# Favor attention and a mixture layer on one core: the sign step keyed to the exp table, two more quarters of GEMM 2 in seven products, another written-out order

## The chip, the core and the metric

The kernel runs on 1 core of a Trainium2 chip. The metric is the device time of one execution in microseconds (us), lower is better. Before the change, three runs gave 1028.66, 1029.24 and 1030.05 us, median 1029.24.

## The reference

Two stages follow each other. Attention with random features: for 8 batches of 8 heads, 576 tokens and 64 channels,

```python
def phi(x):
    proj = np.einsum('bhsd,md->bhsm', x, omega)
    sq = np.sum(x * x, axis=-1, keepdims=True) / 2.0
    h = proj - sq
    h = h - np.max(h, axis=-1, keepdims=True)
    return np.exp(h) / np.sqrt(m)
num = np.einsum('bhsm,bhmd->bhsd', q_p, kv)      # kv = k_p' v, z = sum of k_p
den = np.einsum('bhsm,bhm->bhs', q_p, z)[..., None] + 1e-06
x = num / den
```

and then a two-layer part on the 4608 tokens with 512 channels and 2048 hidden units:

```python
h = x @ w_in
sp = np.maximum(h, 0.0) + np.log1p(np.exp(-np.abs(h)))
g = h * erf(sp)
return g @ w_out
```

Everything is float32; the weights arrive as 64-bit floats.

## The kernel before, in words

**Tiling.** Two heads form a pair; 32 pairs go through attention one after the other (`attention`: projection `ppq`/`ppk`, exponentials `fq`/`fk`, key-value sums `kvp`, transposes `pt` into `qh`, products `nd`, and a division into `xs`). The tokens are cut into six supers (`SUPERS`), 0 and 1 of 2 x 288 columns, 2 to 5 of 2 x 432. A super needs the batches that its tokens lie in, so pairs of later batches run between the matrix products of earlier supers.

**GEMM 1 and GEMM 2.** Each super passes four quarters (`q`) of the hidden units. A quarter is two granules: GEMM 1 fills `hs`, `chain` takes softplus, erf and the product with `hs` (the gate), and GEMM 2 of that quarter follows one quarter later on TensorE, so that GEMM 1 of the next quarter covers the elementwise work. Every float32 product is three matmuls, high x high, high x rest and rest x high. Tiles with h (`xh`, `gh`, `th`, `bh`) hold the high part, those with l the rest. GEMM 1 of supers 0 and 1 is eight plain products (`plain1`), in supers 2 to 5 it is a Strassen-Winograd scheme of seven (`gemm1`, banks `hX`, `hY`, `hZ`). GEMM 2 is plain (`gemm2`, banks `o`) where `blocked(b, q)` is false, and else seven products (`gemm2_blocks`, banks `oX`, `oY`, `oZ`), for which `pieces2` forms differences of the halves of the gated tile (`gs`) and splits seven halves instead of four into high and rest, and `make_sums` forms sums of the weight blocks (`R`, `S`, `c`), once, in the super before the first that needs them.

**Weights.** `make` turns each 64-bit unit (`st`) into high and rest: a sign and exponent step on ScalarE (`w_bias`, a Prelu into `wt`), two integer steps on VectorE, then the high part and the rest into `w`. It stores the result, and later uses fetch it.

**The order.** `build` lists operations with reads, writes, engine choices and due times (`plan`); `Plan.order` is a planner that walks a model clock and gives each engine its next ready operation by due time. What it writes out is each engine's program, and the engines then run in that order with semaphores between them. `JITTER` moves due times within given intervals by a hash; `LAG`, `DRAIN`, `GATES` and others are the planner's lags and dates. On ScalarE a chain takes a lock from its first softplus to its last erf: an operation that names an activation set other than the chain's is held back; one that names none may run in between.

Sections that the change and the prediction touch, by the line numbers of the profile: `FIRST2` and `blocked` (66 to 71), `order` (150), `JITTER` (323), `make` and its `pbias` operation (431, 438), `make_sums` (472), `chain` (790), `pieces2` (828), `gemm2_blocks` (874), `gemm2` (905), `w_bias` (1076). The engines' instructions all carry the line of one helper, L1015, so groups are told apart by tile names.

Of the kernel before, what the change touches and what calls it, by code (L numbers as in the profile page):

```python
# [20 lines left out]
B, H, S, D = 8, 8, 576, 64  # L21
# [41 lines left out]
            ("Y", "S4", "B22", (0, 1), 1),  # L63
            ("X", "A22", "T4", (1, 0), 0))

FIRST2 = (3, 3, 3, 3)


def blocked(b, q):

    return FIRST2[q] <= b < len(SUPERS) - (q == NQ - 1)


COST = dict(mm=0.132, proj=0.222, half=0.156, tr=0.109, kv=1.35, table=1.3)
BANDWIDTH = 270e3
LAG = {"T": 0.32725, "A": 0.2525, "V": 0.2605, "G": 0.3105, "S": 0.2904}
SLOTS = dict(w=8, g=11, u=2, f=2, mx=3, sq=3, v=1, qh=1, ql=1, kh=1, kl=1, xs=12, xh=2, xl=2,
             os=4, ps=8)
CAPS = dict(st=3, wt=1, ws=1, wp=2, cv=2, att=4, moe1=5, moe2=3, hs=4, gs=2, w=6, wsums=7)
# [26 lines left out]
class Plan:  # L106
# [43 lines left out]
    def order(self, slots, caps):  # L150
# [6 lines left out]
        for o in reversed(ops):  # L157
# [2 lines left out]
            for s in o.succ:  # L160
                due = min(due, s.due - dur - 0.4)
            o.due = due
        for k, (lo, hi, amp) in enumerate(JITTER):
            for o in ops:
                if lo <= o.due < hi:
                    o.due += amp * ((o.id * 7919 + k * 104729 + 17) % 1009 / 504.0 - 1.0)
# [45 lines left out]
        while True:  # L212
# [74 lines left out]
            while True:  # L287
                if kind == "idle":
                    idle[x] = True
                elif kind == "done":  # L290
                    for s in x.succ:
                        s.left -= 1
                        lag = 0.0 if x.eng != "S" and len(s.opts) == 1 and s.opts[0][0] == x.eng \
                            else LAG[x.eng]
                        s.ready = max(getattr(s, "ready", 0.0) if s.left >= 0 else 0.0, now + lag) \
                            if hasattr(s, "ready") else now + lag
                        if not s.left:
                            event(max(now, s.ready), "push", s)
                    event(now + LAG[x.eng], "free", x)
                elif kind == "free":  # L300
# [17 lines left out]
def whole_(n):  # L318
# [1 line left out]
    return n < WHOLE or WHOLE2[0] <= n < WHOLE2[1]  # L320


JITTER = ((0, 0, 0), (186.1, 206.1, 4), (0, 0, 0), (0, 0, 0), (0, 0, 0), (227.5, 727.5, 4),
          (648.5, 748.5, 1), (712.0, 762.0, 2), (574.9, 594.9, 8), (27.8, 47.8, 0.5), (390.5, 440.5, 8),
          (458.1, 558.1, 8), (876.3, 896.3, 2), (0, 0, 0), (616.6, 816.6, 1))
AHEAD = 40.56

SPANS = ((0, 288), (288, 288))

DRAIN = 2.0  # L330
DIVIDE = 4.0
WHOLE = 32
WHOLE2 = (0, 0)
LESS = []
ROWS = 8
PAIR = 8.0
FIRST = 11.5
LEAD = 30.0
START0 = 4 * FIRST + 5

GATES = 10.0
RESTS = 6.0
EARLY = (0, 0)
STARTS = ()
BY = 30.0
RPOOL = SPOOL = "g"
VOS = 5
TAIL = [("V", 0.69, -1e9)]
LATE = 40.0
LOADS = 1e9  # L350
GATES0 = 1e9
RESTS0 = 1e9
SQN = 4
SQG = -1e9
SQA = 4.0
WHG = 5.0
WBG = -1e9


def build(emit):  # L360
# [49 lines left out]
    def fetch(u, t, src, ks, n):  # L410
        pl.op("wfetch", [("S", 0.1, AHEAD)], lambda e: E.fetch(t.ap[:, ks[0]:ks[-1] + 1].bitcast(F32), src()),
              reads=[(stored[u], 0)], writes=[(t, (x, k)) for x in "hl" for k in ks],
# [18 lines left out]
    def make(u, t):  # L431

        nm = "_".join(str(c) for c in u)
        st = pl.tile("w", f"st{nm}", [P, HW, 2], I32, "st")
        pl.op("wload", [("S", 0.1, AHEAD)], lambda e: E.w_load(st, u),
              writes=[(st, "h"), (st, "l"), (t, "room")], size=P * HW * 8)
        w = pl.tile("ps", f"wt{nm}", [P, HW], I32, "wp")
        pl.op("pbias", [("A", 0.67, -1e9)], lambda e: E.w_bias(e, st, w),
              reads=[(st, "h")], writes=[(w, 0)])
        pl.op("ptail", TAIL, lambda e: E.w_tail(e, st), reads=[(st, "l")], writes=[(st, "l")])  # L440
        pl.op("pjoin", [("V", 0.68, -1e9)], lambda e: E.w_join(st, w), reads=[(st, "l"), (w, 0)],
              writes=[(w, 0)])
        parts(t, lambda: w.ap.bitcast(F32).rearrange("p (k c) -> p k c", k=2), [(w, 0)], True)
        store(u, t)

    def room():
        count[0] += 1
        if clock[0] < starts[SUMS]:
            return CAPS["w"]
        return CAPS["wsums"] if clock[0] < starts[max(SUMS + 1, *FIRST2)] else SLOTS["w"]  # L450

# [291 lines left out]
    def plain1(b, ph, fp):  # L743
# [5 lines left out]
        def one(i, t):  # L749
# [3 lines left out]
            for k in range(2):  # L753
                product(hp, where[f"A{i + 1}{k + 1}"], b, XPLAIN, f"B{k + 1}{t + 1}", k, k)
            pl.op("hout", [("A", d["A"], -1e9), ("V", d["V"], 0.0)],
                  lambda e: E.h_out(e, hs.ap[:, i, t, :], hp, T), reads=[(hp, 0)], writes=[(hs, (i, t))],
                  plan=clock[0] + DRAIN)
        return [lambda i=i, t=t: one(i, t) for i in range(2) for t in range(2)]
# [7 lines left out]
    def gemm1(b, ph, fp, where, srcs, which):  # L766
# [5 lines left out]
        def one(bank, wn, xn, to, plus):  # L772
# [6 lines left out]
            if plus:  # L779
                pl.op("hadd", [("V", d["V"], -1e9)], lambda e: E.h_add(hs.ap[:, to[0], to[1], :], hp, T),  # L780
                      reads=[(hp, 0), (hs, to)], writes=[(hs, to)], plan=clock[0] + DRAIN)
            else:
                pl.op("hout", [("A", d["A"], -1e9), ("V", d["V"], 0.0)],
                      lambda e: E.h_out(e, hs.ap[:, to[0], to[1], :], hp, T), reads=[(hp, 0)],
                      writes=[(hs, to)], plan=clock[0] + DRAIN)
        return [lambda x=x: one(*x) for x in PRODUCTS]
# [87 lines left out]
    def gemm2_blocks(b, q, j, where, srcs):  # L874
# [6 lines left out]
        def one(bank, wn, xn, to, plus):  # L881
# [10 lines left out]
            if plus or q:  # L892
                pl.op("oadd", [("V", d["V"], -1e9)], lambda e: E.o_add(o, op, t, T),
                      reads=[(op, 0), (o, t)], writes=[(o, t)], plan=clock[0] + DRAIN)
            else:
                pl.op("oout", [("V", d["V"], -1e9), ("A", d["A"], -1e9)],
                      lambda e: E.o_out(e, o, op, t, T), reads=[(op, 0)], writes=[(o, t)],
                      plan=clock[0] + DRAIN)
            if q == NQ - 1 and (to[0] == 0 and wn == "S4" or wn == "A22"):
# [5 lines left out]
    def gemm2(b, q, et):  # L905
# [7 lines left out]
        def out(t):  # L913
            if q == 0:
                pl.op("oout", [("V", d["V"], -1e9), ("A", d["A"], -1e9)],
                      lambda e: E.o_out(e, o, ops[t], t, T), reads=[(ops[t], 0)], writes=[(o, t)],
                      plan=clock[0] + DRAIN)
            else:
# [3 lines left out]
        def one(t, f):  # L922
            if not ops:
                ops.extend(pl.tile("ps", f"o{b}_{q}_{et}_{i}", [P, 512], F32, "moe2",
                                   6 if b == len(SUPERS) - 1 else None) for i in range(2))
                w.append(weights2(q // 2, et, q % 2))
                if b == FIRST2[q] - 1:
                    beside[q, et] = w[0]
# [448 lines left out]
```

## Time and profile before

| | |
|---|---|
| median of 3 runs | 1029.24 us (1028.66 to 1030.05) |
| the profiled execution's own time | 1027.2 us |
| its span, first to last instruction | 1025.4 us |
| TensorE matmul busy | 1003.5 us, 98% |
| VectorE, ScalarE, GpSimd busy | 795.0, 688.5, 612.9 us |
| mean granted TensorE clock | 0.997 of 2.4 GHz |

PE is TensorE's matmul row, PEld its weight loads, DVE is VectorE, ACT ScalarE, POOL GpSimd, SP the engine that issues the DMAs. Busy TensorE time takes in overlap of matmuls, so what one costs is read from how far its starts lie apart. Idle time of an engine counts only where it ends something that TensorE waits for.

### The profile page before, as it was taken

What the parts mean: (1) busy time and instruction counts of PE and PEld (TensorE: products, weight loads), DVE (VectorE), ACT (ScalarE), POOL (GpSimd) and SP (SyncE); (2) the same over time, 40 slices, a digit from 0 to 9 for tenths busy, and PEclk for the clock granted to TensorE, in tenths of its full rate; (3) what the DMA queues carried; (4) which work ended last, traced back from release to release, by engine and by line L of the source; (5) the groups of instructions that cost most, each with busy time, mean ns of one, the idle gap of its engine ahead of it and who ended that gap; (6) DMA issues with size and microseconds to landing.
All of it is one profiled execution on the core that took longest, in us unless ns stands there. A gap on an engine that the chain in (4) does not pass through costs nothing.

```text
span 1025.4 us, 19428 instructions
## 1 busy us (share of the span) xinstructions
PE 1003.5 (98%) x7132; PEld 932.8 (91%) x7132; DVE 795.0 (78%) x1284; ACT 688.5 (67%) x1295; POOL 612.9 (60%) x446
## 2 busy tenths in 40 slices
PE   8999999999999999999999999999999999999998
PEld 7799889999999999999999888989989999989997
DVE  5788878877876976677787987798887687678664
ACT  8988776787685774765768585677657655644650
POOL 3625443875567816455788356489884668957520
PEclk9999999999999999999999999999999999999999
DMA  8377776699686766676657866656786457686751
GB/s 229 90 267 237 255 239 244 240 320 307 218 298 205 255 213 220 225 243 202 223 187 277 280 224 214 226 199 212 246 278 223 164 185 227 219 288 219 230 180 70
DMA packets 99486, 232.72 MB, mean 227 GB/s; under 512 B 11200, under 2 KB 11712, under 8 KB 99392
## 3 DMA queue, kind: packets, MB, share of 16 engines
q1 hardware_dynamic: 99232, 231.42, 67.5%
q8 instruction: 57, 0.93, 0.4%
q14 instruction: 37, 0.30, 0.1%
q10 hardware_dynamic: 160, 0.07, 0.0%
HBM read 188.45 MB, written 42.99 MB: 226 GB/s over the span
## 4 chain that ended last, share of the span: by engine, by line
PE 84%; DVE 6%; issue 3%; ACT 2%; DMA 2%; POOL 1%; SPq 1%; POOLq 0%; DVEq 0%; ACTq 0%
PE o L1015 17%; PE hX L1015 13%; PE h L1015 10%; PE oX L1015 9%; PE hY L1015 6%; PE nd L1015 5%; PE oY L1015 4%; PE ppq L1015 4%; PE ppk L1015 4%; PE kvp L1015 4%; PE hZ L1015 3%; PE pt L1015 2%; PE oZ L1015 2%; DMA uq<-qT 1%; DVE gs L1015 1%
## 5 line engine op out<-in xcount | busy, mean ns | idle before, releaser
L1015 PE MATMUL o<-gh,w 128*128 128x288 f32 (+1 forms) x832 | 213.5, 329 | 0.6 <-DVE w L1015 0.6
L1015 POOL TENSOR_TENSOR hs<-gs,hs 128x864 f32<-128x864 f32 (+1 forms) x50 | 112.2, 2266 | 106.1 <-ACT gs L1015 85.2
L1015 PE MATMUL hX<-xh,wb 128*128 128x432 f32 x512 | 168.6, 369 | 2.4 <-ACT hs L1015 1.4
L1015 PEld LDWEIGHTS o<-gh,w 128*128 128x128 f32 x832 | 145.2, 188 | 6.4 <-DVE w L1015 1.2
L1015 PE MATMUL o<-gl,w 128*128 128x288 f32 (+1 forms) x416 | 132.9, 319 | 0.1
L1015 PE MATMUL h<-xh,w 128*128 128x288 f32 x512 | 127.9, 318 | 5.0 <-DVE w L1015 4.4
L1015 PEld LDWEIGHTS hX<-xh,wb 128*128 128x128 f32 x512 | 96.2, 188 | 8.6 <-ACT hs L1015 1.8
L1015 POOL TENSOR_TENSOR uq<-uq 128x288 f32<-128x288 f32 (+1 forms) x50 | 50.9, 1038 | 79.2 <-DMA uq<-qN 38.9
L1015 PEld LDWEIGHTS h<-xh,w 128*128 128x128 f32 x512 | 89.0, 193 | 9.5 <-DVE w L1015 5.6
L1015 ACT ACT_TABLE_LOAD x72 | 92.4, 1283 | 2.0 <-PEq L1368 0.7
L1015 PE MATMUL hX<-xl,wb 128*128 128x432 f32 x256 | 91.6, 358 | 0.0
L1015 ACT ACTIVATE fk<-ppk,mxk 128x128 f32<-128x128 f32 x288 | 81.2, 379 | 8.9 <-DVE mxk L1015 8.0
L1015 PE MATMUL hY<-xh,wb 128*128 128x432 f32 x256 | 84.8, 368 | 0.0
L1015 ACT ACTIVATE fq<-ppq,mxq 128x128 f32<-128x128 f32 x288 | 78.1, 386 | 8.2 <-DVE mxq L1015 7.9
L1015 PE MATMUL oX<-th,wb 128*128 128x432 f32 x264 | 82.9, 361 | 0.0
L1015 PEld LDWEIGHTS o<-gl,w 128*128 128x128 f32 x416 | 78.3, 188 | 2.7 <-DVE gl L1015 0.5
L1015 ACT ACTIVATE rc<-nd,eps 64x288 f32<-64x288 f32 x128 | 63.4, 496 | 25.2 <-PE nd L1015 22.2
L1015 ACT ACTIVATE hs<-hX 128x432 f32<-128x432 f32 x71 | 37.1, 529 | 63.2 <-PE hX L1015 62.3
L1015 PE MATMUL nd<-qh,kh 128*128 128x288 f32 x256 | 76.3, 410 | 1.9 <-DVE qh L1015 1.4
L1015 PE MATMUL h<-xl,w 128*128 128x288 f32 x256 | 76.9, 300 | 0.7 <-POOL xl L1015 0.7
L1015 DVE TENSOR_TENSOR xs<-nd,rc 64x288 f32<-64x288 f32 (+1 forms) x160 | 61.2, 393 | 16.6 <-ACT rc L1015 11.1
L1015 ACT ACTIVATE gs<-hs 128x1728 f32<-128x1728 f32 (+1 forms) x48 | 69.4, 1481 | 1.1 <-POOL bl L1015 0.8
(141 smaller groups left out, 2642.4 us busy)
## 6 DMA issues: line engine op xcount, KB each, us to landing
wb<-wdc SPq DMA_DIRECT2D x216, 256.0 KB, 3.6
wb<-wdw SPq DMA_DIRECT2D x162, 256.0 KB, 3.9
w<-wdw SPq DMA_DIRECT2D x52, 512.0 KB, 4.7
st<-w SPq DMA_DIRECT2D x32, 512.0 KB, 4.9
wdw<-w SPq DMA_DIRECT2D x32, 512.0 KB, 4.3
wdc<-c SPq DMA_DIRECT2D x32, 512.0 KB, 4.7
v<-vP SPq DMA_DIRECT2D x32, 325.0 KB, 5.2
uk<-kR SPq DMA_DIRECT2D x24, 320.0 KB, 3.9
```

The costliest lines, as they stand in the source:

```text
L1015: return tc.keep_in_program_order(method(*args, **kwargs))
```

## The change

Three things. The sign step (`pbias`) names the set "exp", so the planner no longer puts it between softplus and erf. `FIRST2` for quarters 2 and 3 goes from 3 to 2: GEMM 2 of super 2 takes seven products in these quarters too, and the weight sums that they need are formed in super 1 and no longer in super 2. And the table of numbers that shifts due times, with the planner's lags and dates, is another one; each of its entries now carries its own key, and the start of the two-layer part is the number 51.0, which is what the formula gave before.

```diff
-FIRST2 = (3, 3, 3, 3)
+FIRST2 = (3, 3, 2, 2)
...
-LAG = {"T": 0.32725, "A": 0.2525, "V": 0.2605, "G": 0.3105, "S": 0.2904}
+LAG = {"T": 0.33914999999999995, "A": 0.258, "V": 0.24975, "G": 0.2994, "S": 0.3024}
...
-        for k, (lo, hi, amp) in enumerate(JITTER):
+        for lo, hi, amp, k in JITTER:
...
-JITTER = ((0, 0, 0), (186.1, 206.1, 4), (0, 0, 0), (0, 0, 0), (0, 0, 0), (227.5, 727.5, 4),
...
-AHEAD = 40.56
+JITTER = ((186.1, 206.1, 4, 581), (227.5, 727.5, 4, 5), (648.5, 748.5, 1, 6), (712.0, 762.0, 2, 7),
...
+AHEAD = 40.09
...
-DRAIN = 2.0
-DIVIDE = 4.0
+DRAIN = 2.08
+DIVIDE = 3.94
...
-START0 = 4 * FIRST + 5
-
-GATES = 10.0
-RESTS = 6.0
+START0 = 51.0
+
+GATES = 8.94
+RESTS = 5.64
...
         pl.op("pbias", [("A", 0.67, -1e9)], lambda e: E.w_bias(e, st, w),
-              reads=[(st, "h")], writes=[(w, 0)])
+              reads=[(st, "h")], writes=[(w, 0)], set="exp")
```

Three places of the written-out order. First, ScalarE's program around the third chain of super 0 (`gs0_4` and `gs0_5` are its two tiles, written from `hs` by softplus and then in place by erf; `wt...<-st...` is the sign step). Before:

```order
L1015 ACTIVATE hs0_1_1_1579<-h110_1_1_1708 128x288
L1015 ACT_TABLE_LOAD
L1015 ACTIVATE gs0_4_1779<-hs0_1_0_1481 128x1152
L1015 ACT_TABLE_LOAD
L1015 ACTIVATE wt2_0_3_1_1811<-st2_0_3_1_1693 128x512
L1015 ACT_TABLE_LOAD
L1015 ACTIVATE gs0_5_1780<-hs0_1_1_1579 128x1152
L1015 ACTIVATE w2_0_3_1_20_1694<-wt2_0_3_1_1811 128x2x256
L1015 ACT_TABLE_LOAD
L1015 ACTIVATE gs0_4_1779<-gs0_4_1779 128x1152
L1015 ACTIVATE gs0_5_1780<-gs0_5_1780 128x1152
L1015 ACTIVATE wt1_1_4_1885<-st1_1_4_1764 128x512
```

With the change:

```order
L1047 ACTIVATE hs0_1_1_1589<-h110_1_1_1729 128x288
L1047 ACT_TABLE_LOAD
L1047 ACTIVATE gs0_4_1779<-hs0_1_0_1561 128x1152
L1047 ACTIVATE gs0_5_1780<-hs0_1_1_1589 128x1152
L1047 ACT_TABLE_LOAD
L1047 ACTIVATE gs0_4_1779<-gs0_4_1779 128x1152
L1047 ACTIVATE gs0_5_1780<-gs0_5_1780 128x1152
L1047 ACT_TABLE_LOAD
L1047 ACTIVATE wt2_0_3_1_1865<-st2_0_3_1_1688 128x512
L1047 ACTIVATE wt1_1_4_1885<-st1_1_4_1772 128x512
```

The sign step of `wt2_0_3_1` moves behind the last erf; the two table loads on either side of it are gone, and the load of the exp set now follows the last erf directly. The second chain (`gs0_2`, `gs0_3`) changes in the same way. Over the whole program ScalarE has 72 table loads before and 68 now.

Second, TensorE's program where GEMM 1 of super 0, quarter 2 (banks `h000_1_0`, `h000_1_1`) first uses the weight units `w1_1_0` and `w1_1_2`. Before:

```order
L1015 MATMUL h000_1_0_1451<-xh0_1_658,w1_1_0_13_1262 128x288
L1015 MATMUL ppk_1_3_0_1477<-wqk_70,uk_1_3_1105 128x128 x3
L1015 MATMUL ppk_1_3_1_1485<-wqk_70,uk_1_3_1105 128x128 x3
L1015 MATMUL ppk_1_3_2_1492<-wqk_70,uk_1_3_1105 128x128 x3
L1015 MATMUL pt_1_2_0_1500<-ident_67,fq_1_2_1287 128x128 x3
L1015 MATMUL pt_1_2_1_1516<-ident_67,fq_1_2_1287 128x128 x3
L1015 MATMUL h000_1_1_1523<-xh0_0_526,w1_1_2_15_1386 128x288
```

With the change:

```order
L1047 MATMUL nd_1_2_0_0_1532<-qh_1_2_1450,kh_1_2_1322 128x288
L1047 MATMUL nd_1_2_1_0_1535<-qh_1_2_1450,kh_1_2_1322 128x288
L1047 MATMUL nd_1_2_0_1_1537<-qh_1_2_1450,kh_1_2_1322 128x288
L1047 MATMUL h000_1_0_1501<-xh0_0_526,w1_1_0_13_1248 128x288
L1047 MATMUL h000_1_0_1501<-xl0_0_555,w1_1_0_13_1248 128x288
L1047 MATMUL h000_1_0_1501<-xh0_0_526,w1_1_0_13_1248 128x288
L1047 MATMUL h000_1_0_1501<-xh0_1_656,w1_1_0_13_1248 128x288
L1047 MATMUL h000_1_0_1501<-xl0_1_668,w1_1_0_13_1248 128x288
L1047 MATMUL h000_1_0_1501<-xh0_1_656,w1_1_0_13_1248 128x288
L1047 MATMUL nd_1_2_1_1_1555<-qh_1_2_1450,kh_1_2_1322 128x288
L1047 MATMUL h000_1_1_1563<-xh0_0_526,w1_1_2_15_1446 128x288
```

The projection and the transposes come earlier than this piece, and the four `nd` products of that pair now stand before the first use of `w1_1_2`.

Third, TensorE's program where GEMM 2 of super 2, quarter 2 starts. Before, it is plain:

```order
L1015 MATMUL hY2_1_3_6086<-xh2_0_4437,wb99_5999 128x432
L1015 MATMUL hY2_1_3_6086<-xl2_0_4472,wb99_5999 128x432
L1015 MATMUL hY2_1_3_6086<-xh2_0_4437,wb99_5999 128x432
L1015 MATMUL o2_2_0_0_6195<-gh2_4_5960,w2_1_0_0_101_6046 128x432
L1015 MATMUL o2_2_0_0_6195<-gl2_4_5983,w2_1_0_0_101_6046 128x432
L1015 MATMUL o2_2_0_0_6195<-gh2_4_5960,w2_1_0_0_101_6046 128x432
L1015 MATMUL hX2_1_2_5995<-xh2_0_4437,wb100_6020 128x432
```

With the change:

```order
L1047 MATMUL oX2_2_0_6262<-bb2_2_6068,wb101_6098 128x432 x6
L1047 MATMUL nd_4_3_0_0_6278<-qh_4_3_6212,kh_4_3_5928 128x288
L1047 MATMUL nd_4_3_1_0_6283<-qh_4_3_6212,kh_4_3_5928 128x288
L1047 MATMUL oX2_2_1_6287<-bb2_2_6068,wb101_6098 128x432 x3
L1047 MATMUL nd_4_3_0_1_6294<-qh_4_3_6212,kh_4_3_5928 128x288
L1047 MATMUL oY2_2_0_6297<-th2_2_0_6109,wb102_6119 128x432
L1047 MATMUL oY2_2_0_6297<-tl2_2_0_6222,wb102_6119 128x432
```

The plain products (96 matmuls in a quarter) give way to products on block `bb`, then on the differences `th`, `tl` (84 in a quarter). Over the whole program TensorE has 2748 matmuls of 432 columns before and 2724 now; all other kinds keep their number.

## Rows read from the trace of the kernel before

**Rows 1.** The page, busy time of each engine over the span.

```profile
PE 1003.5 (98%) x7132; PEld 932.8 (91%) x7132; DVE 795.0 (78%) x1284; ACT 688.5 (67%) x1295; POOL 612.9 (60%) x446
```

**Rows 2.** Who TensorE waited for, whole span: us in total, times, longest.

```profile
PE h L1015 <- DVE w L1015: 4.4, 4, 2.2
...
PE pt L1015 <- DVE hs L1015: 1.9, 1, 1.9
...
PE hX L1015 <- ACT hs L1015: 1.4, 1, 1.4
PE hX L1015 <- DVE hs L1015: 1.0, 1, 1.0
```

**Rows 3.** Stages: length, busy (instructions) PE, PEld, DVE, ACT, POOL, clock, DMA.

```profile
114.90:118.30 3.40, 3.40 (x14) 3.12 (x14) 3.23 (x5) 1.81 (x4) 3.40 (x4) 0.50 0.96 354
...
155.90:159.30 3.40, 3.40 (x16) 3.40 (x15) 3.26 (x8) 2.47 (x6) 0.25 (x1) 0.50 0.95 329
```

**Rows 4.** ScalarE's timeline, second and third chain: start, duration, operation, idle before.

```profile
94.45 1.28 ACT L1015 ACT_TABLE_LOAD   x1
95.75 1.17 ACT L1015 ACTIVATE gs<-hs 128x1152 f32<-128x1152 f32 x1
...
104.05 2.22 ACT L1015 ACTIVATE gs<-gs 128x1152 f32<-128x1152 f32 x2
...
109.10 1.27 ACT L1015 ACTIVATE wt<-st 128x512 f32<-128x512 f32 x2
...
133.64 1.28 ACT L1015 ACT_TABLE_LOAD   x1
...
142.32 2.23 ACT L1015 ACTIVATE gs<-gs 128x1152 f32<-128x1152 f32 x2
144.45 0.62 ACT L1015 ACTIVATE wt<-st 128x512 f32<-128x512 f32 x1
```

**Rows 5.** TensorE's timeline, waits between 104 and 160 us, the releaser behind the arrow.

```profile
113.55 0.40 PE L1015 MATMUL h<-xh,w 128*128 128x288 f32 x1 [2.18 <-DVE w L1015]
...
148.56 0.40 PE L1015 MATMUL h<-xh,w 128*128 128x288 f32 x1 [0.78 <-DVE w L1015]
...
150.99 0.91 PE L1015 MATMUL pt<-ident,fq 128*128 128x128 f32 x6 [0.56 <-DVE qh L1015]
...
152.99 0.40 PE L1015 MATMUL h<-xh,w 128*128 128x288 f32 x1 [0.60 <-ACT qh L1015]
...
154.80 0.54 PE L1015 MATMUL h<-xh,w 128*128 128x288 f32 x2 [1.28 <-DVE w L1015]
```

**Rows 6.** The chain that ended last, its longest unbroken run of matmuls of 432 columns.

```profile
1003.46 17.68 PE o L1015 x90
```

**Rows 7.** Groups of elementwise instructions by form: count, busy, mean ns, idle before.

```profile
L1015 DVE TENSOR_TENSOR os<-oX,os 128x432 f32<-128x432 f32 x70 | 41.5, 602 | 22.9 <-PE oX L1015 22.7
...
L1015 ACT ACTIVATE th<-gs 128x1728 fp32r<-128x1728 f32 x17 | 28.0, 1648 | 24.6 <-DVE gs L1015 14.1 <-DVE bl L1015 8.2 <-POOL gs L1015 2.3
...
L1015 DVE TENSOR_TENSOR tl<-gs,th 128x1728 fp32r<-128x1728 f32 x10 | 27.7, 2769 | 0.8 <-POOL th L1015 0.4 <-ACT th L1015 0.3
```

**Rows 8.** The stretches that hold super 1 and the last half of super 2, columns as in rows 3.

```profile
205.00:370.00 165.00, 164.35 (x1420) 153.52 (x1419) 126.09 (x240) 119.04 (x269) 106.94 (x98) 1.00 0.78 263
...
470.00:560.00 90.00, 90.00 (x614) 82.50 (x613) 69.58 (x116) 61.58 (x118) 64.10 (x51) 1.00 0.63 222
```

**Rows 9.** TensorE: four `nd` products in a row, and one between other matmuls.

```profile
24.50 2.25 PE L1015 MATMUL nd<-qh,kh 128*128 128x288 f32 x8
...
121.29 0.65 PE L1015 MATMUL nd<-qh,kh 128*128 128x288 f32 x2
121.56 0.51 PE L1015 MATMUL h<-xh,w 128*128 128x288 f32 x1
```

**Rows 10.** Operations on tile `gs`: count, shortest, median and longest in ns, first and last start.

```profile
L1015 DVE TENSOR_TENSOR gs<-hs,gs x17: 1051/1698/2898, 561.5 to 968.3; 128x864 f32<-128x864 f32 x17
...
L1015 DVE TENSOR_TENSOR tl<-gs,th x10: 1948/2470/5477, 569.0 to 979.5; 128x1728 fp32r<-128x1728 f32 x10
```

More of the change, by code (lines that the diff above doesn't have):

```diff
@@ L320, in whole_ @@
     return n < WHOLE or WHOLE2[0] <= n < WHOLE2[1]
-JITTER = ((0, 0, 0), (186.1, 206.1, 4), (0, 0, 0), (0, 0, 0), (0, 0, 0), (227.5, 727.5, 4),
-          (648.5, 748.5, 1), (712.0, 762.0, 2), (574.9, 594.9, 8), (27.8, 47.8, 0.5), (390.5, 440.5, 8),
-          (458.1, 558.1, 8), (876.3, 896.3, 2), (0, 0, 0), (616.6, 816.6, 1))
-AHEAD = 40.56
+JITTER = ((186.1, 206.1, 4, 581), (227.5, 727.5, 4, 5), (648.5, 748.5, 1, 6), (712.0, 762.0, 2, 7),
[34 rows of a table added]
+AHEAD = 40.09
 SPANS = ((0, 288), (288, 288))
-DRAIN = 2.0
-DIVIDE = 4.0
+DRAIN = 2.08
+DIVIDE = 3.94
 WHOLE = 32
@@ L336 @@
 PAIR = 8.0
-FIRST = 11.5
+FIRST = 11.4
 LEAD = 30.0
-START0 = 4 * FIRST + 5
-GATES = 10.0
-RESTS = 6.0
+START0 = 51.0
+GATES = 8.94
+RESTS = 5.64
 EARLY = (0, 0)
 STARTS = ()
-BY = 30.0
+BY = 30.39
 RPOOL = SPOOL = "g"
@@ L348 @@
 TAIL = [("V", 0.69, -1e9)]
-LATE = 40.0
+LATE = 52.68
 LOADS = 1e9
@@ L354 @@
 SQG = -1e9
-SQA = 4.0
-WHG = 5.0
+SQA = 6.0
+WHG = 4.28
 WBG = -1e9
```

34 rows, old and new, of the table JITTER are left out of this document.

## Prediction

> **What bounds the kernel now.** I read the page first: TensorE is busy 1003.5 us, 98% of the span, and no other engine passes 78% [rows 1]. So the time is TensorE's work plus its holes, and a change counts by the matmuls it takes out and the holes it closes or opens. The list of waits on TensorE names the holes: the largest sum is 4.4 us in four waits of GEMM 1 on weights that VectorE finishes (`h` <- `w`) [rows 2]. The table of stages tells where these cost twice: in two stretches of 3.4 us the granted clock is 0.50, so TensorE runs at 1.2 instead of 2.4 GHz, and 14 and 16 matmuls are recorded there [rows 3]. Each lies behind a hole of the timeline: the wait of 2.18 us that ends at 113.55, and the four waits of 0.78, 0.56, 0.60 and 1.28 us between 148 and 155 [rows 5]. The reader is to see that these holes follow the second and the third chain on ScalarE: the first table load of a chain starts at 94.45 and at 133.64, the erf of both tiles starts only at 104.05 and 142.32, and the sign steps that the late weights need at 109.10 and 144.45 [rows 4].
>
> **Term 1, the products.** Two quarters go from 96 to 84 matmuls: 24 fewer of 432 columns. An unbroken run takes 17.68 us for 90, 0.196 us each [rows 6]. 24 x 0.196 = 4.7 us, all on TensorE, which is the bound: **-4.7 us**.
>
> **Term 2, the sign step.** Four table loads go, 1.28 us each [rows 4]: 5.1 us of ScalarE, none of it on the path by itself. What they give is read at the two places. Third chain, new order by old durations: two loads, two softplus of 1.17, erf 2.23: 7.1 us from the first load to the end of erf, against 142.32 + 2.23 - 133.64 = 10.9 before, so the gates start 3.8 us earlier; the sign step of `w1_1_4` comes after one more load and one sign step of 0.62, at 9.0 us instead of 144.45 - 133.64 = 10.8. The waits here are 0.78 to 1.28 us, and all shorter than what is gained: I count the four as closed, 3.2 us, and with them the half-speed stretch. Half speed over 3.4 us costs 1.7 us, since the same matmuls take half of it at full speed. Second chain: erf ends over 4 us earlier (the same 7.1 us and a short copy that stays inside, against 104.05 + 2.22 - 94.45 = 11.8). But in the new order the sign step of `w1_1_2` stands behind more of ScalarE's work than before, while TensorE asks for that weight later too, behind the four `nd`. The trace shows neither distance, so I bound: the hole of 2.18 us and its half-speed stretch of 1.7 either stay, 0, or go, 3.9; nearest is the third chain, where what comes behind erf gains under 2 us, and I put 1.6. Sum: 3.2 + 1.7 + 1.6 = 6.5. **-6.5 us**, between nothing (both holes come back elsewhere) and the 5.4 us of waits in this stretch [rows 5] plus 2 x 1.7, 8.8.
>
> What a load costs is a place where page and trace differ. Between the end of the exponentials at 94.44 and the start of softplus at 95.75 lie 1.31 us, the load and nothing more [rows 4]. The Trainium skill, "ScalarE: Activation LUTs", section "What ACT_TABLE_LOAD costs", gives 1283 ns for the load and adds a drain of some 1380 ns to every switch, 2.66 us in all; by it the four loads would be 10.6 us of ScalarE and term 2 would tend to its upper end. This trace shows the 1283 and no drain.
>
> **Term 3, the added elementwise work.** A new quarter needs four differences of 864 columns (1.70 us each on VectorE [rows 10]), high parts and rests of three more halves (1.5 x 1.65 and 1.5 x 2.77) and six more results to add (0.60 each) [rows 7]: 6.8 + 2.5 + 4.2 + 3.6 = 17.1 us, 34 for both, in the stretch from 470 to 560 us. There VectorE is free for 20.4 us, ScalarE for 28.4 and GpSimd for 25.9 [rows 8], 74.7 together, so it fits, and GEMM 1 of the next quarter covers it as it does in supers 3 to 5. What that cover leaves open is read from these: behind the start of GEMM 2 in seven products the waits on `hs` are 1.9, 1.4 and 1.0 us [rows 2], 4.3 us in eleven quarters, 0.4 each. **+0.8 us**, between nothing and 4.3. The sums of the weights for these quarters move from super 2 into super 1, where the three engines leave 38.9, 46.0 and 58.1 of 165 us [rows 8]; I cost the move at nothing. If that cover is gone, the fetch of the sums is late in super 2. Transfers: 28 more fetches of single blocks and 8 fewer of double units; at a DMA share of 0.63 to 0.78 [rows 8] that is nothing too.
>
> **Term 4, the rest of the new order.** Its programs differ nearly everywhere past the first attention pairs. One thing can be counted: an `nd` product behind another takes a fourth of some 2 us, 0.48, one between other matmuls 0.27 [rows 9], and 38 instead of 49 stand behind one another; that is 2.3 us, of which 30 more changes between kinds of matmul take back a part. I take **-1.0 us**, between +1 and -2.3. The waits outside of the two places, 4.3 us on `hs`, I leave as they are: the same producers are as late elsewhere.
>
> Sum: -4.7 - 6.5 + 0.8 - 1.0 = -11.4 us. The profiled execution took 1027.2 us, so 1015.8; the median of the runs stands 2.0 above it, which gives **1017.8 us**.
>
> **Rivals.** *The holes move.* The sign steps leave the stretch but queue behind it; the weights stay late, which the bound of term 2 allows, and only the matmuls are saved: 1029.2 - 4.7 + 0.8 = 1025.3 us. For it: ScalarE's work up to there is only 5 us shorter and `w1_1_2` has more ahead of it there. Against: the gates come 4 us earlier at both chains, for certain.
>
> *The order closes nearly everything.* All waits of the two places and the 4.3 us on `hs` behind them go: 1029.2 - 4.7 - 8.8 - 4.3 - 2.3 = 1009.1 us. For it: at its longest a wait behind 160 us is 1.9 us, and small shifts can close such a one. Against: in so tight a program a shift also opens some.
>
> *VectorE is held up by GpSimd, slower.* The same subtraction takes VectorE from 1.05 to 2.90 us, and the rest of a difference block from 1.95 to 5.48 [rows 10]: at the longest it is held 1.8 and 3.5 us. Seven-product quarters lean on just these, and by the count of the new program GpSimd writes 60 pieces of difference blocks instead of 30. If two blocks of each new quarter are held that long, they come 2 x 5.3 = 10.6 us late in a quarter; the products on two other blocks, 24 matmuls or 4.7 us, cover a part, so TensorE waits 5.9 us in each, and each such hole brings a half-speed stretch of 1.7: 15.2 us. With the holes of before unchanged that is 1025.3 + 15.2 = 1040.5 us. It decides when the last difference block is ready more than 4.7 us after its turn. For it: VectorE and GpSimd together are busy 133.7 us in 90 [rows 8]. Against: eleven such quarters run now, and wait 4.3 us in all [rows 2]. The Trainium skill, "SBUF — State Buffer", section "SBUF: two separate sides", has the cause: VectorE and GpSimd share one pair of ports by an exclusive lock and the loser stands still. The spread of these two rows agrees with it.
>
> *The change doesn't do what it says.* The loads of the middle of a chain might not come from the sign step. The written-out order has 68 instead of 72 and the matmuls are counted, so this has next to no chance; the time would be 1029.
>
> **How the numbers follow.** Forecast 0.60, holes move 0.20, everything closes 0.10, VectorE held up 0.09, no effect 0.01. A measurement of this kernel can tell about 0.2%, 2.1 us, from no change. The forecast and the closing order are faster by more, and most of the second case (1025.3, with 2 us to the bound); the rest of it, the last case and the milder part of the hold-up fall within 0.2%. So faster 0.86, same 0.06, slower 0.08. The range takes the forecast with its bounds, term 2 from 0 to 8.8, term 3 up to 4.3, and reaches to the closing order below and past the moved holes above: 1008 to 1027 us.
>
> **What would show it.** Right: no table load between two softplus of one chain, 68 in all; no stretch at half clock between 100 and 165 us, or one at most; waits of `h` on `w` under 2 us in sum; `oX` and `oY` in super 2; the number of matmuls records down by 24. Term 3 is wrong if TensorE waits on `th`, `tl` or `gs` work in the new quarters, or on `wb` at their start. Wrong altogether: a half-speed stretch in a new place, or a sum of waits on TensorE that has not fallen from what the list shows.

## The result, and the profile after

| | before | with the change |
|---|---|---|
| median of 4 runs each, taken side by side | 1028.95 us | 1015.56 us (1014.17 to 1016.23) |
| ratio of the two | | 0.9876, 95% interval 0.986 to 0.9891 |
| the profiled execution's own time, its span | 1027.2, 1025.4 us | 1015.25, 1013.4 us |
| TensorE's waits in the list, sum | 16.9 us | 14.1 us |
| table loads on ScalarE | 72 | 68 |

The change makes the kernel faster by 1.24%, 12.8 us. Of the four runs of "The numbers of the order alone" below, the profiled one took 2798.84 us, with a granted clock of 0.16 from 643 us on, and the ratio given there leaves it out.

The page of the changed kernel, busy time of each engine:

```profile
PE 995.4 (98%) x7108; PEld 926.1 (91%) x7108; DVE 788.7 (78%) x1278; ACT 695.3 (69%) x1307; POOL 636.1 (63%) x477
```

Against [rows 1] TensorE has 24 matmuls less and 8.1 us less of busy time. GpSimd has 23 us more, and TensorE waits for none of it directly, as the next list shows; what it does to VectorE comes in the last section. Who TensorE waited for over the whole span (us in total, times, longest):

```profile
PE ppk L1047 <- ACT uk L1047: 3.9, 1, 3.9
PE nd L1047 <- DVE qh L1047: 2.9, 5, 1.1
PE o L1047 <- DVE w L1047: 1.8, 3, 1.0
PE o L1047 <- ACT w L1047: 1.5, 2, 0.7
PE h L1047 <- ACT w L1047: 1.0, 1, 1.0
PE hX L1047 <- DVE xl L1047: 0.7, 1, 0.7
...
PE h L1047 <- DVE w L1047: 0.2, 1, 0.2
```

This answers to [rows 2]. The 4.4 us of `h` on VectorE's `w` are 0.2, and the 4.3 us on `hs` behind 385 us are gone: behind 385 us this list has no wait at all. What is new stands in the third and fourth line: `o` on `w`, 2.8 us of it between 104 and 160 us, where the kernel before has no such wait. They are four waits of GEMM 2. The fifth line, `h` on `w` from ScalarE, is an old wait in a new form. TensorE's timeline of the five:

```profile
107.13 0.40 PE L1047 MATMUL o<-gh,w 128*128 128x288 f32 x1 [0.72 <-ACT w L1047]
...
108.62 0.40 PE L1047 MATMUL o<-gh,w 128*128 128x288 f32 x1 [0.95 <-DVE w L1047]
...
144.28 0.40 PE L1047 MATMUL o<-gh,w 128*128 128x288 f32 x1 [0.74 <-ACT w L1047]
...
145.19 0.53 PE L1047 MATMUL o<-gh,w 128*128 128x288 f32 x2 [0.38 <-DVE w L1047]
...
152.28 0.40 PE L1047 MATMUL h<-xh,w 128*128 128x288 f32 x1 [0.99 <-ACT w L1047]
```

The weights of the first four are `w2_0_3_0` and `w2_0_3_1`, the two whose sign steps the change moved behind the chains. The fifth is the first use of `w1_1_6`. By the two written-out orders the kernel before waited for this weight too: the waits of 0.60 and 1.28 us behind 152 us [rows 5] are its first use and its rest. The rest was late there by VectorE, which did a shift for another weight between the join and the rest:

```profile
151.82 1.60 DVE L1015 TENSOR_SCALAR st<-st 128x512 int32<-128x512 int32 x1
...
154.06 0.68 DVE L1015 TENSOR_TENSOR w<-wt,w 128x512 fp32r<-128x512 f32 x1
```

By stretch, TensorE's waits were 6.2 us up to 104, 5.8 from 104 to 160, 0.6 from 160 to 385 and 4.3 behind that; now they are 6.6, 4.3, 3.2 and 0.

ScalarE's third chain, to be read against the second half of [rows 4]:

```profile
132.69 1.28 ACT L1047 ACT_TABLE_LOAD   x1
133.98 2.23 ACT L1047 ACTIVATE gs<-hs 128x1152 f32<-128x1152 f32 x2
136.23 1.28 ACT L1047 ACT_TABLE_LOAD   x1
137.52 2.23 ACT L1047 ACTIVATE gs<-gs 128x1152 f32<-128x1152 f32 x2
139.76 1.28 ACT L1047 ACT_TABLE_LOAD   x1
141.06 1.21 ACT L1047 ACTIVATE wt<-st 128x512 f32<-128x512 f32 x2
```

From the first load to the end of erf it takes 7.1 us instead of 10.9, and to the end of `w1_1_4`'s sign step 9.6 instead of 11.4. Of the two half-clock stretches of [rows 3] this execution has one, in another place; and the last half of super 2, now with two quarters in seven products, answers to the second of [rows 8] (columns as there):

```profile
109.50:112.90 3.40, 3.40 (x17) 3.38 (x16) 2.71 (x6) 1.49 (x6) 3.14 (x4) 0.50 0.79 257
470.00:560.00 90.00, 90.00 (x613) 82.29 (x612) 72.28 (x118) 65.64 (x122) 64.55 (x45) 1.00 0.71 235
```

### The profile page after: what moved, and what is told of

It reads as the page before. It is cut to its first block, busy times and chain, and to the rows that moved or that the text cites. A ratio compares the mean times of both kernels' runs of the same rounds, so it can differ in the third digit from the quotient of the medians.

```text
span 1013.4 us, 19460 instructions
## 1 busy us (share of the span) xinstructions
PE 995.4 (98%) x7108; PEld 926.1 (91%) x7108; DVE 788.7 (78%) x1278; ACT 695.3 (69%) x1307; POOL 636.1 (63%) x477
## 4 chain that ended last, share of the span: by engine, by line
PE 88%; DVE 6%; DMA 4%; ACT 1%; SPq 1%; issue 1%; DVEq 0%; ACTq 0%
PE hX L1047 15%; PE o L1047 14%; PE oX L1047 12%; PE h L1047 8%; PE hY L1047 7%; PE oY L1047 6%; PE nd L1047 5%; PE ppq L1047 4%; PE hZ L1047 4%; PE ppk L1047 3%; PE kvp L1047 3%; PE oZ L1047 3%; PE pt L1047 2%; DMA st<-w 2%; DVE st L1047 1%; DMA uk<-kT 1%
## 5 line engine op out<-in xcount | busy, mean ns | idle before, releaser
L1047 PE MATMUL o<-gh,w 128*128 128x288 f32 (+1 forms) x704 | 176.0, 324 | 3.3 <-DVE w L1047 1.8
L1047 POOL TENSOR_TENSOR hs<-gs,hs 128x864 f32<-128x864 f32 (+1 forms) x44 | 95.5, 2190 | 94.5 <-ACT gs L1047 83.0
L1047 PEld LDWEIGHTS o<-gh,w 128*128 128x128 f32 x704 | 122.4, 189 | 8.2 <-DVE w L1047 2.5
L1047 PE MATMUL h<-xh,w 128*128 128x288 f32 x512 | 123.4, 312 | 2.2 <-ACT w L1047 1.0
L1047 PE MATMUL o<-gl,w 128*128 128x288 f32 (+1 forms) x352 | 110.3, 313 | 0.0
L1047 PE MATMUL oX<-th,wb 128*128 128x432 f32 x312 | 101.4, 364 | 0.0
L1047 POOL TENSOR_TENSOR uq<-uq 128x288 f32<-128x288 f32 (+1 forms) x50 | 45.7, 934 | 72.8 <-DMA uq<-qN 31.8
L1047 PE MATMUL hY<-xh,wb 128*128 128x432 f32 x256 | 88.2, 372 | 0.0
L1047 ACT ACTIVATE hs<-hX 128x432 f32<-128x432 f32 x64 | 33.8, 531 | 67.4 <-PE hX L1047 63.3
L1047 POOL TENSOR_TENSOR tl<-gs,th 128x864 fp32r<-128x864 f32 x32 | 71.1, 2241 | 9.7 <-ACT th L1047 3.5
```

Source lines behind the costliest of these rows:

```text
L1047: return tc.keep_in_program_order(method(*args, **kwargs))
```

## The experiments

All ratios are against the kernel before, run on the same chip in turns; the medians of before differ by up to 0.2% from one set of runs to the next (1026.66 to 1028.95 us), so ratios are compared and not times. A first set takes single parts of the change with every other instruction in its place. A second plans the list anew for a part. A third tries to close what the changed kernel still waits for.

### One part at a time, the rest of the order as it was

**24 matmuls left out.** In the kernel before, one of the three products of 24 units in the two quarters of super 2:

```diff
             for x, (l, r) in enumerate(((wh, gh.ap), (wh, gl.ap), (wl, gh.ap))):
+                if x == 1 and op.name[:4] in ("o2_2", "o2_3") and (fi == 1 or fi == 2 and op.name[5] in "01"):
+                    continue
```

> The kernel before with 24 of the 192 matmuls of the two quarters of super 2 left out (of each of 24 units the product of the weight's high part with the gate's rest), not one other instruction moved or added. It measures term 1 by itself. Theory (the bound is TensorE's work): 24 x 0.196 = 4.7 us less, 3.7 to 5.2. Rival (the work beside TensorE sets the pace in super 2, and the holes take up what the matmuls leave): 0 to 2.5 us less, with new waits of o or nd behind 360 us.

Measured: 0.9957 (0.9941 to 0.9973), 4.4 us less. The page has the 24 records less, and the waits by stretch stay (6.3, 5.9, 0.5, 4.8 us). Term 1 holds.

**The chains alone.** In the kernel before, the two softplus and the two erf of chains 2 and 3 are put together in the written-out list:

```diff
-    for o in plan.order(slots, CAPS):
+    listed = plan.order(slots, CAPS)
+    for m in (2, 3):
+        mine = [o for o in listed if o != "table" and o.macro == m]
+        i = listed.index(mine[0])
+        listed = [o for o in listed if o not in mine]
+        listed[i:i] = mine
+    for o in listed:
```

> The kernel before with one thing altered: in chains 2 and 3 the two softplus and the two erf stand together behind the first load, the sign steps out of their stretch, every other engine's order as before (68 loads, 7132 matmul records). Theory (term 2 of the prediction): the loads and the late sign steps open the holes from 104 to 160 us; the waits of h on w there fall from 4.4 us to under 2, at least one of the two half-clock stretches goes, and the time falls by 3 to 8.8 us against the kernel before, to some 1022. Rival (the holes move): the gates come early, but the weights of the sign steps that now stand behind the chain are as late as before; waits and half-clock stretches stay, and the time falls by 0 to 2 us.

Measured: 0.9973 (0.9957 to 0.999), 2.8 us less. With its interval of 1.0 to 4.4 us the time alone decides nothing: 2.8 lies between what the rival and what the theory expects. The waits tell more, TensorE's waits from 104 to 160 us:

```profile
PE h L1015 <- DVE w L1015: 1.6, 3, 0.9
PE o L1015 <- DVE w L1015: 1.0, 2, 0.5
PE o L1015 <- ACT w L1015: 0.7, 1, 0.7
PE h L1015 <- ACT qh L1015: 0.5, 1, 0.5
```

`h` on `w` falls under 2 us as the theory wants, and the two lines of `o` on `w` are what the rival wants: the same two weights as in the changed kernel. Their sign steps stand elsewhere than in the change, though: right behind the last erf and ahead of the next load. The edit also puts the copies `kh` behind erf, which costs a wait of 1.3 us at 103 that the change does not have; over the whole span the listed waits fall only from 16.9 to 16.0 us. Both half-clock stretches between 104 and 160 us are gone, and one stands where before had none:

```profile
760.00:762.00 2.00, 2.00 (x9) 1.85 (x8) 1.97 (x5) 0.98 (x2) 1.92 (x2) 0.66 0.89 339
762.00:764.00 2.00, 2.00 (x8) 1.80 (x7) 0.67 (x3) 0.80 (x2) 2.00 (x2) 0.50 0.01 3
```

**Four loads put back.** In the changed kernel, between the two softplus of chains 2 and 3:

```diff
...
+    for m in (2, 3):
+        j = [n for n, o in enumerate(listed) if o != "table" and o.name == "sp" and o.macro == m][1]
+        listed.insert(j, "table")
...
```

> The changed kernel with four table loads put back: in chains 2 and 3 the set of exp is loaded between the two softplus and softplus's set again (72 loads), with no other instruction moved. It tells the price of the loads alone. Theory of term 2: 2.6 us of ScalarE per chain on the path of the gates and of the sign steps behind erf; the waits from 104 to 160 us, 4.3 us now, grow by 3 to 5 us, a second half-clock stretch (1.7 us) comes back, and the time rises by 3 to 7 us over the changed kernel. Rival: the loads are covered by other work, 0 to 2 us.

Measured: 0.9928 (0.9905 to 0.995); the changed kernel itself, repeated as a control, gave 0.9881 (below), so the loads cost 0.0047, 4.8 us. The two intervals lie only 0.0003 apart, so this price may be off by some 3 us. In the third chain they stand like this:

```profile
133.30 1.17 ACT L1047 ACTIVATE gs<-hs 128x1152 f32<-128x1152 f32 x1
134.49 2.57 ACT L1047 ACT_TABLE_LOAD   x2
137.07 1.17 ACT L1047 ACTIVATE gs<-hs 128x1152 f32<-128x1152 f32 x1
```

The waits from 104 to 160 us are 7.3 us, and nearly all the growth is in one line, the same two weights again:

```profile
PE o L1047 <- ACT w L1047: 5.5, 2, 3.9
```

So 5.1 us of loads on ScalarE become about as much time, since what waits behind them is on the path. This is the price of the loads in term 2 seen from the other side. The profile has one half-clock stretch, behind the later of these waits, and not the two that the theory expects. The Trainium skill, "ScalarE: Activation LUTs", section "What ACT_TABLE_LOAD costs", would add a drain of some 1380 ns to every switch of sets. These three rows show none: the next softplus starts 0.01 us behind two loads of 2.57 us together.

**Three places on VectorE and ScalarE.** The kernel before, three instructions put behind a short one (`behind` takes the first operation out of the written-out list and sets it right behind the second):

```diff
...
+    behind("rest", "bl4_0", "hadd", "hZ4_0_3")
+    behind("high", "th5_0_0", "hout", "hX5_0_3", 1)
+    behind("rest", "bb5_2", "hout", "hX5_1_3")
...
```

> The kernel before with three instructions put behind a short one that they stood ahead of: the rest bl of 3.87 us at 759 and the rest bb of 2.95 us at 971 on VectorE, the high part th of 1.65 us at 908 on ScalarE, each behind the copy or the addition of a half hs that TensorE waits for there. It tells whether the waits on hs, which the prediction left as they are, are a matter of place in the list alone. Theory (they are): the three waits, 4.3 us in sum, fall under 1 us, and the time by 3 to 4.5 us. Rival (bl, bb and th are then late by as much, since the engines have no room): new waits on th, tl, bb or os of 2 us and more, the time within 1.5 us of the kernel before.

Measured: 0.9952 (0.9933 to 0.9971), 4.9 us less. The first place on VectorE's timeline, in the kernel before:

```profile
759.01 3.87 DVE L1015 TENSOR_TENSOR bl<-hs,bh 128x1728 fp32r<-128x1728 f32 x1
762.80 0.59 DVE L1015 TENSOR_TENSOR hs<-hZ,hs 128x432 f32<-128x432 f32 x1
```

And with the edit:

```profile
758.92 0.59 DVE L1015 TENSOR_TENSOR hs<-hZ,hs 128x432 f32<-128x432 f32 x1
760.07 0.61 DVE L1015 TENSOR_TENSOR hs<-hZ,hs 128x432 f32<-128x432 f32 x1 [0.56 <-PE hZ L1015]
760.60 2.70 DVE L1015 TENSOR_TENSOR bl<-hs,bh 128x1728 fp32r<-128x1728 f32 x1
```

VectorE now waits 0.56 us for the bank and adds it at once, instead of first doing the `bl` of 3.87 us. The three waits of [rows 2] on `hs` shrink to one:

```profile
PE hX L1015 <- DVE hs L1015: 0.9, 1, 0.9
```

No other change was made, and no new wait on the moved `bl`, `th` or `bb` came for it: 3.4 of these 4.3 us hung on the place in the list alone. The gain of 4.9 us (3.0 to 6.9) is larger than the waits that went; what gave the rest was not read.

### One part, the list planned anew

**The products alone.** `FIRST2 = (3, 3, 2, 2)` in the kernel before, with its own numbers for the order.

> The kernel before with only the two quarters of super 2 set to seven products; its own table of the order, so the list is planned anew and differs in many places. 24 matmuls less: 4.7 us by the rows. Theory: the products alone give 4.7 us, some 1024 us, give or take some 2 us for the holes that the new list opens or closes, 72 loads as before. Rival (the added elementwise work is not covered): waits of TensorE on hs, th, tl or gs in the stretch from 470 to 560 us, and a time less than 2.5 us under the kernel before.

Measured: 1.0031 (1.0008 to 1.0053), 3.2 us more, where the matmuls by themselves are worth 4.4 less. TensorE's timeline in the new quarters:

```profile
517.32 0.46 PE L1015 MATMUL hY<-xh,wb 128*128 128x432 f32 x1 [1.29 <-DVE os L1015]
...
523.28 0.55 PE L1015 MATMUL pt<-ident,fq 128*128 128x128 f32 x3 [1.30 <-DVE qh L1015]
524.70 1.72 PE L1015 MATMUL nd<-qh,kh 128*128 128x288 f32 x6 [0.87 <-DVE qh L1015]
```

So VectorE is late there, 3.5 us in 8 us of the new quarters. Whether the added work does that, or the place that these numbers give to other instructions, no run separates; behind 385 us the waits are 8.7 us in all, against 4.3 before.

**The sign step's set alone.** `set="exp"` in the kernel before.

> The kernel before with the sign step's rule alone (it may not run in softplus's stretch), the list planned anew with the numbers of before: 68 loads. Theory of term 2 by itself: 3 to 6.5 us less. Rival (numbers picked for one program do not fit another, as the three runs above with a list planned anew show, which stand 8 to 18 us above what their parts would give): 2 to 18 us above the kernel before, with the holes behind 160 us.

Measured: 1.0044 (1.0022 to 1.0065), 4.5 us more: the rival. The 68 loads are there, from 104 to 160 us the waits are 4.3 us, the same as in the changed kernel, and other places pay (of the first line 2.5 us lie behind 160 us):

```profile
PE o L1015 <- DVE w L1015: 4.6, 3, 2.5
PE hX L1015 <- DVE hs L1015: 4.3, 2, 2.4
```

**The numbers of the order alone**, in the kernel before.

> The kernel before with the changed kernel's numbers for the order alone (the jitter list, the lags, the fixed date of the MoE part), without the sign step's set and with two quarters of super 2 in six... nine products as before: 7132 matmuls, loads inside the chains. If the new numbers close the holes behind 385 us by themselves (4.3 us to 0), the time is 2 to 5 us under the kernel before. Rival: the numbers fit only the program that they were picked for, and on this one they close nothing: 0 to 8 us above the kernel before.

Measured: 1.0177 (1.0146 to 1.0208), 18 us more. Its three runs have mean granted clocks of 0.990 to 0.993, against 0.995 to 0.998 in the kernel before; by that difference some 6 of the 18 us are clock, an estimate. Where the rest goes was not read.

**The changed kernel without the products.** `FIRST2 = (3, 3, 3, 3)` in it.

> The changed kernel with the two quarters of super 2 back in nine products, all else the same, so 24 matmuls more: 4.7 us by the rows. Theory of terms 1 and 3 (the products are worth their matmuls and the rest is covered): 4 to 6 us above the changed kernel. Rival (the numbers of the order fit only the program that they were picked for): 7 to 12 us above it, with waits on hs, os or qh behind 385 us that the changed kernel does not have.

Measured: 1.0109 (1.0062 to 1.0156), 2.3% above the changed kernel's 0.9881, some 23 us where 24 matmuls are 4.7. The first line of its list of waits is one that the changed kernel does not have:

```profile
PE hX L1047 <- DVE hs L1047: 5.3, 4, 2.7
```

The profiled execution is 18.2 us longer than that of the changed kernel (1031.6 against 1013.4 us of span). Of these the matmuls are 4.7, the waits 9.4 (23.5 against 14.1 us, 8.3 of them behind 385 us) and a second half-clock stretch 1.7; 2.4 stay open.

So none of the four can be read as the worth of its part. The numbers of the order go with one program, and each list that is planned with numbers of another costs some 7 to 19 us more than its part would give (4.5 + 2.8 for the set, 3.2 + 4.4 for the products, 23.5 - 4.7 for the last, and 18 for the numbers alone).

### What the changed kernel still waits for

**A control.** The changed kernel again, beside the runs that follow.

> The changed kernel itself, unaltered, on the chip of the next runs, so that they can be set against it on one chip: 0.9876 of the kernel before, give or take 0.3%. If it stands 0.3% or more away, the chip and not the edit explains differences of that size.

Measured: 0.9881 (0.9859 to 0.9902). The waits of `o` on `w` are the same to 0.1 us. The stretch at half clock behind them is not there; it ran like this:

```profile
108.50:111.90 3.40, 3.40 (x29) 3.40 (x28) 3.37 (x7) 2.02 (x7) 3.40 (x4) 1.00 0.95 203
```

**Sign steps earlier.** In the changed kernel the sign steps of `w2_0_3_0`, `w2_0_3_1` and `w1_1_4` go right behind the last erf of their chains, ahead of the load:

```diff
...
+    for m, names in ((2, ("wt2_0_3_0",)), (3, ("wt1_1_4", "wt2_0_3_1"))):
+        for name in names:
+            o = listed.pop(place("pbias", name))
+            i = next(n for n, x in enumerate(listed) if x != "table" and x.name == "erf!" and x.macro == m)
+            listed.insert(i + 1, o)
...
```

> The changed kernel with the sign steps of w2_0_3_0 (chain 2) and of w2_0_3_1 and w1_1_4 (chain 3) moved up to right behind the last erf, ahead of the next load of the set of exp (still 68 loads; two slots of PSUM trade places so that it can be). Theory: what TensorE now waits for at 107, 108 and 144 us is the moved sign step itself, which stands behind a load and the exponentials; ahead of them these waits, 3.2 us in all, shrink to under 1 us, and with them the half-clock stretch (1.7 us) goes: 2.5 to 4.6 us less than the changed kernel, 1011 to 1013 us. Rival: the exponentials, the gates or the next weight are then late by as much, and the time stays within 1.5 us of the changed kernel's.

Measured: 0.9902 (0.9878 to 0.9926), no gain. The wait for the join's result has hardly moved:

```profile
105.89 0.40 PE L1047 MATMUL o<-gh,w 128*128 128x288 f32 x1 [0.49 <-ACT w L1047]
107.38 0.54 PE L1047 MATMUL o<-gh,w 128*128 128x288 f32 x2 [0.96 <-DVE w L1047]
```

The sign step is done at 99.96 in this run, and the weight is late all the same. VectorE's timeline of the changed kernel, in which the order of these steps is the same, says why:

```profile
96.74 0.42 DVE L1047 TENSOR_SCALAR st<-st 128x512 int32<-128x512 int32 x1
...
104.15 1.69 DVE L1047 TENSOR_SCALAR st<-st 128x512 int32<-128x512 int32 x1
105.76 0.69 DVE L1047 SCALAR_TENSOR_TENSOR wt<-wt,st 128x512 int32<-128x512 int32 x1
106.36 1.01 DVE L1047 TENSOR_REDUCE mxk<-ppk 128x3 f32<-128x384 f32 x2
107.29 0.68 DVE L1047 SCALAR_TENSOR_TENSOR wt<-wt,st 128x512 int32<-128x512 int32 x1
107.88 0.68 DVE L1047 TENSOR_TENSOR w<-wt,w 128x512 fp32r<-128x512 f32 x1
```

The first line is the tail of `w2_0_3_0` itself, its join the line at 105.76. The join stands behind the tail of a later weight (104.15), and the rest at 107.88 behind two reductions and another join. A list of waits names the last writer, here `w` from ScalarE; the queue that made it late is a step further back, on VectorE.

**Joins earlier too.** On top of the last edit (`shift` sets the first operation ahead of the second, or behind it with a 1); the load of chain 3 also moves behind these steps.

```diff
...
+    shift("pjoin", "wt2_0_3_0", "high", "gh0_2")
...
+    shift("prest", "wt2_0_3_0", "ptail", "st1_1_1")
+    shift("pjoin", "wt2_0_3_1", "gate", "hs0_1_1")
+    shift("phigh", "wt2_0_3_1", "high", "gh0_4", 1)
+    shift("prest", "wt2_0_3_1", "ptail", "st1_1_4")
...
```

> The changed kernel with the sign steps of chains 2 and 3 early as in the run before, and now also the later steps of the two late weights w2_0_3_0 and w2_0_3_1 early: the join on VectorE ahead of the gates' last cast or product, the high part on ScalarE ahead of the exponentials or the query halves, the rest on VectorE ahead of the next weight's tail; in chain 3 the load of the set of exp behind those. Theory (VectorE's order in these places, not ScalarE's sets, now makes the two weights late): the waits of o on w at 106 to 109 and 143 to 145 us, 2.5 to 2.9 us in sum, go to under 0.6, and the time falls by 2 to 4 us against the changed kernel. Rival (the gates are as late as the weights, or the next weights are late in turn): new waits on gh, h on w or fk of the same sum, and a time within 1.5 us of it.

Measured: 0.9887 (0.9867 to 0.9907), no gain: the rival. The waits of `o` on `w` from 104 to 160 us are gone, all of them, and others have come or grown, 5.2 us in sum against 4.7 in the control; two of them:

```profile
PE nd L1047 <- ACT fk L1047: 1.9, 1, 1.9
PE h L1047 <- ACT w L1047: 1.4, 1, 1.4
```

**Nine tails left out.** In the changed kernel; the joins take the high words instead, so that they cost the same.

```diff
...
+        if o != "table" and o.name == "ptail" and o.uses[0].name in UNTAILED:
+            continue
...
```

> The changed kernel with the tails (a shift of 512 columns on VectorE, 0.4 to 1.9 us each) of the nine weights joined from 100 to 155 us left out; their joins take the high words in place of the tails. Theory (VectorE's queue holds the weights that TensorE waits for from 104 to 160 us): the waits there, 4.3 to 4.7 us, fall under 2.5, and the time by 2 to 4 us against the changed kernel. Rival (ScalarE's chain and the landing of st hold them): the waits stay over 3.5 us and the time falls by less than 1.2 us.

Measured: 0.9882 (0.9855 to 0.9909), no gain, and 3.5 us of waits from 104 to 160 us. Less work on VectorE takes one wait away (0.72 at 107), and `h` on `w` at 152 us stays at 1.0. Ahead of that one stands a landing, as ScalarE's timeline of this run shows; the line is the sign step of `w1_1_6`:

```profile
149.19 0.63 ACT L1048 ACTIVATE wt<-st 128x512 f32<-128x512 f32 x1 [1.38 <-DMA st<-w]
```

In the changed kernel ScalarE waits 0.43 us for the same landing. So the three runs agree with one account: in this stretch VectorE's queue, ScalarE's queue and the landing of `st` are late by about the same, and where one is relieved the next is there. The sum of the waits stays between 3.5 and 5.2 us. The landing itself was not relieved in any run, so its share is not shown. None of the three variants is faster than the change. The three edits on the kernel before (the 24 matmuls, the chains, the three places) were not put together in one.

## Why the prediction was right, and where its terms were not

The forecast was 1017.8 us and the measured time 1015.56, inside the range and on the side that was given 0.86. The sum of 11.4 came out at 12.0 between the two spans and 13.4 between the medians; most of that difference is not the kernel's, since the 2.0 us that the prediction sets the median above the profiled execution were 0.3 in the changed kernel. That the sum is so near is partly luck: term 2 is too large by 3.3 us and term 4 too small by about as much, with opposite signs.

**Term 1, -4.7.** Right. The records are 24 less, and the matmuls alone are worth 4.4 us (2.8 to 6.1 by the interval).

**Term 2, -6.5.** Right in its mechanism, and about twice what came out. The times along ScalarE came out as worked out, 7.1 us to the end of erf, and `h` on `w` fell from 4.4 to 1.2 us. The step that failed is "I count the four as closed, 3.2 us, and with them the half-speed stretch". The waits on `w1_1_4` (0.78 us) and on `pt` (0.56) closed. The other two were on `w1_1_6`, and neither followed the chain alone: its rest stood behind a shift of 1.60 us on VectorE, and it is still waited for, 0.99 and 0.22 us. And the sign steps that were moved out of the chains belong to weights that TensorE needs too, and these were now late: 2.8 us of `o` on `w`. The waits of the stretch went from 5.8 to 4.3, and one half-clock stretch of 1.7 us went: 3.2 us. The chains alone gave 2.8 with a wait of 1.3 that the edit itself brought, and the four loads put back cost 4.8. So *the holes move* was part of what happened, not another way in which it could go. The stretch at 109.50 is also, by the letter, the prediction's own sign of being wrong altogether, "a half-speed stretch in a new place", while its signs of being right, "one at most" and a sum of waits that falls (16.9 to 14.1 us), held. The price of 1.7 us for such a stretch was firmer in the text than it is: the control has the same waits at 107 and 108 and no such stretch, and the changed kernel, matmul against matmul, is 1.5 us later than the control at the end of the stretch than at its start, 0.8 of which come back a few us on, where the control waits and it does not.

**Term 3, +0.8.** It came out as nothing: no wait behind 385 us, and none on `th`, `tl`, `gs` or `wb` anywhere. But "so it fits" was shown for this list only. With the products alone and the list planned with other numbers, VectorE was late in the new quarters by 3.5 us. Free time of the engines in a stretch, 20.4 us on VectorE there [rows 8], is needed for cover and does not give it.

**Term 4, -1.0.** Too small, and this is what made up for term 2. The step is "The waits outside of the two places, 4.3 us on `hs`, I leave as they are: the same producers are as late elsewhere". The producers were not late for lack of time. A short addition stood behind a long `bl`, `th` or `bb` that nobody was waiting for, and three such moves alone gave 4.9 us. The new list closes these and opens 2.6 us from 160 to 385 us and 0.4 up to 104, so 1.3 of it are left as waits. The sum of waits and clock leaves 2.8 of the 12.0 us of span: -4.7 matmuls, -2.8 waits, -1.7 clock. Part of it lies in the `nd`, for which the prediction had put 1.0 with a bound of 2.3: from the starts of the matmuls in the two traces, waits and half-clock stretches left out, the 256 `nd` cost 47.3 us instead of 48.5, some 1 us less. The other 1.6 to 1.8 us were not located, and no run separates them.

**The other rivals.** *VectorE is held up by GpSimd* did not happen, though GpSimd does write 60 pieces of difference blocks: the waits that it needs are not there. *The order closes nearly everything* happened behind 385 us and nowhere else. That the numbers of the order fit only their own program, 7 to 19 us for each part that is planned with numbers of another, was not among the rivals; it did not bear on this change, which brought its numbers with it.

Added up, the three edits on an unchanged list give 4.4 + 2.8 + 4.9 = 12.1 us, each good to some 2 us, next to the 12.8 of the change. That is no proof of completeness, since the change also opens holes that they do not, but it names where the time came from: less work on TensorE, the chains kept whole, and short instructions no longer behind long ones.

## What to carry to other kernels

Where a wait in a tuned list is on an engine with free time, look at what stands ahead of the producer in its queue before calling it a limit: a long instruction that nobody waits for, moved behind a short one that TensorE does wait for, is the cheapest of all changes. A step that is moved off one path lands on another, so ask who needs the moved step's own result, and follow a wait back past the last writer to the queue that held it. And a part of a change to a kernel whose order is picked by numbers can be priced only by an edit that leaves the list as it is; planned anew, each part looks like a loss.

## What the runs showed of the hardware

Half-clock stretches come and go behind the same waits. The granted clock was 0.50 for 3.4 us behind the waits of 0.72 and 0.95 us in the profile of the changed kernel, and 1.00 behind the same two waits in the control. In the kernel before it stayed at 1.00 behind the wait of 1.9 us at 763, and behind that same wait it fell to 0.50 in the run with the chains alone. Of the ten runs with the chains alone, five have a mean granted clock of 1.000, the others of 0.998 and 0.999. So whether the clock falls cannot be read from the waits alone, and where it fell in the changed kernel 1.5 us were lost and 0.8 of them came back.

A shift of 512 columns on VectorE took 0.42 us at 96.74, where GpSimd was idle, and 1.69 us at 104.15, where it multiplied gates until 105.55:

```profile
98.91 3.38 POOL L1047 TENSOR_TENSOR uq<-uq 64x576 f32<-64x576 f32 x2 [6.60 <-DMA uq<-qT]
102.36 3.19 POOL L1047 TENSOR_TENSOR hs<-gs,hs 128x576 f32<-128x576 f32 x2
```

The second shift was over 0.3 us behind that multiplication. By the Trainium skill, "SBUF — State Buffer", section "SBUF: two separate sides", the two engines share a pair of ports by an exclusive lock: whoever starts first has it for its whole instruction, and the other stands still. The two rows agree with it; whether this shift is one of the operations that need the pair, no run here says. Here it held up a join on TensorE's path, a stretch that the prediction's rival had not looked at.
